# Retention and a PReLU network on one core: attention re-tiled into units of 256 tokens by four heads

## The chip, the cores and the metric

The kernel runs on one NeuronCore of a Trainium2 chip. The metric is the device time of one execution in microseconds (us), the median of several runs. Profiled executions are one run each, and all readings of a trace are from such a run. PE is TensorE (the matrix engine), PEld its weight loads, DVE VectorE, ACT ScalarE, POOL GpSimd and SP SyncE, which here only issues DMAs.

## The reference

Inputs q, k, v are [4 batches, 8 heads, 768 tokens, 64]; w_in is [512, 2048], w_out [2048, 512], alpha [2048]; all float32. For each batch and head a recurrent retention is computed, and its output, heads side by side, goes through a two-layer network:

```python
gamma = 1.0 - 2.0 ** (-5.0 - np.arange(H))
scale = 1.0 / np.sqrt(D)
for t in range(S):
    state = gamma * state + k[t] (outer) v[t]      # per batch and head, 64 x 64
    y[t] = scale * q[t] @ state
x = y laid out as [3072 tokens, 512]
h = x @ w_in
out = (max(h, 0) + alpha * min(h, 0)) @ w_out      # [3072, 512]
```

(The loop is written in short; the index of batch and head is left out.)

## The kernel before, in words

The recurrence is cut into chunks of 128 tokens. Within a chunk the product is a masked attention (scores k.q, mask, times v); from chunk to chunk a 64x64 state per head is carried. A **unit** is one chunk with all eight heads, 24 units in all; four units make a **block** of 512 tokens, six blocks. The network runs block by block.

- `load` (L99, DMA at L104) brings k, q and v of a unit, 256 KB each, 128 tokens on 128 partitions, in pieces of 64 floats (256 bytes), all issued on SP's queue.
- `prep` (L119) scales k (L122) and q (L130) by powers of gamma into float16, and copies v (L142). From unit 10 on, the transposed k and q (tile kq) come from a DMA transpose (L138) on SP's queue; earlier units are transposed on PE (L159) and copied by ACT (L166).
- `stage_a` forms the state sums (L172, tile stp), adds them to the decayed state (L184, or L188 for a batch's first chunk, on DVE) and decays it for the next chunk (L190, POOL, tile tg).
- `stage_b` forms the scores (L205): a head has 64 rows, so two heads' matmuls run on the two row halves of the array, each with 128 columns of weights. DVE masks them (L215, tile m).
- `stage_c` forms the output (L230, L237, and L245 for the carried state, all 128-row products in which half of each weight tile is zero), and ACT copies it into xT (L255).
- `ffn1` (L266) is the first product (L273, 16 tiles of four matmuls with 512 columns), with relu(-h) on ACT (L283, tile hm) and the combination on DVE (L284, tile gt). `ffn2` (L303) is the second (L312, four groups of 16 matmuls), evicted by ACT (L321) and written to the output by a DMA that ACT issues (L325), 128 rows of 2 KB.

The order of the work is written out by hand. Each engine runs its own instructions in program order, and a scheduler doesn't move them. `ffn1` and `ffn2` are generators; `tick(gen, m)` issues the next m of their matmuls, and between ticks the stages of the next block's units are issued. In the steady part (n from 1), the next block's preps and later loads are issued during `ffn1(n)`, its attention during `ffn2(n)`. In the opening, block 0's attention stands alone; `ffn1(0)` starts on three of four units; the weights come through POOL's queue (L384, L388), and the loads of blocks 1 and 2 are held until the second piece of w_out has landed (`held`, L109). `keep_busy` (L328, L332) is 64 small matmuls without use for the result, put before block 1's attention. PSUM has eight banks: four under tag pa, four under tag pb.

Of the kernel before, what the change touches and what calls it, by code (L numbers as in the profile page):

```python
# [9 lines left out]
FP = mybir.dt.float32  # L10
# [8 lines left out]
def kernel(  # L19
# [9 lines left out]
):  # L29
    nc = tc.nc  # L30
# [4 lines left out]
    C = 128  # L35
    NCH = S // C
    NU = B * NCH
    UB = 4
    NBLK = NU // UB
    TB = UB * C  # L40
    scale = 1.0 / np.sqrt(D)
    g64 = 1.0 - 2.0 ** (-5.0 - np.arange(H, dtype=np.float64))
    p_ar = np.arange(128, dtype=np.float64)


# [3 lines left out]
    for h in range(H):  # L49
        tab_np[:, h] = g64[h] ** (127.0 - p_ar)  # L50
        tab_np[:, H + h] = scale * g64[h] ** (p_ar + 1.0 - 128.0)
    for p in range(NP):
        tab_np[0:64, 2 * H + p] = g64[2 * p] ** 128
        tab_np[64:128, 2 * H + p] = g64[2 * p + 1] ** 128
    tab_np[0:NFT, NTAB - 16 : NTAB] = np.eye(NFT)
    tab_np = tab_np.astype(np.float32)
    mi_np = np.zeros((128, 256), dtype=np.float16)
    mi_np[:, 0:128] = p_ar[:, None] <= p_ar[None, :]
    mi_np[:, 128:256] = np.eye(128)
# [9 lines left out]
    mi = sbp.tile([128, 256], F16, tag="mi", name="mi")  # L69
    mask = mi[:, 0:128]  # L70
    ident = mi[:, 128:256]
# [3 lines left out]
    w_in_all = sbp.tile([128, 4, d_ff], F16, tag="win", name="win")  # L75
    w_out_all = sbp.tile([128, NFT, d_model], F16, tag="wout", name="wout")


    NV = 8
    NPE = 10  # L80
    vext = [
        sbp.tile([128, NP, 4, 64], F16, tag=f"vx{i}", name=f"vx{i}")[:, :, 0:3, :]
        for i in range(NV)
    ]

    NT = 2
    sst = [sbp.tile([128, NP, 128], FP, tag=f"ss{i}", name=f"ss{i}") for i in range(NT)]
    tgs = {}

    def ps(name, dt=FP, n=512, tag="pa"):  # L90
        return psp.tile([128, n], dt, tag=tag, bufs=4, name=name)


    staged = {}
    prepped = {}

    held = []

    def load(u):  # L99
        b, c = divmod(u, NCH)  # L100
        t = {}
        for nm, src in (("k", k), ("q", q), ("v", v)):
            t[nm] = sbp.tile([128, H, D], FP, tag=f"{nm}s", bufs=8, name=f"{nm}s{u}")
            ins = nc.sync.dma_start(  # L104
                out=t[nm],
                in_=src[b, :, C * c : C * c + C, :].rearrange("h p d -> p h d"),
            )
            if held:
                tc.add_manual_dep(  # L109
                    ins.ins,  # L110
                    held.pop().ins.name,
                    mybir.DependencyInfo(
                        mybir.DependencyClass.Sync, mybir.DependencyReason.DATA
                    ),
                    reason="loads of the second block after the weights",
                )
        staged[u] = t

    def prep(u, between=None):  # L119
        t = staged.pop(u)  # L120
        kdq = sbp.tile([128, 2, H, D], F16, tag="kdq", bufs=8, name=f"kdq{u}")
        (nc.vector if u < 2 * UB else nc.gpsimd).tensor_tensor(  # L122
            out=kdq[:, 0],
            in0=t["k"],
            in1=tab[:, 0:H].unsqueeze(2).to_broadcast([128, H, D]),
            op=MULT,
        )
        if between:
            between()
        nc.gpsimd.tensor_tensor(  # L130
            out=kdq[:, 1],
            in0=t["q"],
            in1=tab[:, H : 2 * H].unsqueeze(2).to_broadcast([128, H, D]),
            op=MULT,
        )
        kq = sbp.tile([128, 2 * NP, 128], F16, tag="kq", bufs=8, name=f"kq{u}")
        if u >= NPE:
            nc.sync.dma_start_transpose(  # L138
                out=kq, in_=kdq.rearrange("p a h d -> p (a h d)")
            )  # L140
        vx = vext[u % NV]
        nc.gpsimd.tensor_copy(  # L142
            out=vx[:, :, 0::2, :],
            in_=t["v"].rearrange("p (a b) d -> p a b d", b=2),
        )
        prepped[u] = (kdq, kq, vx)


    live = {}
    xT = {}  # L150

    def stage_a(u):
        b, c = divmod(u, NCH)
        kdq, kq, vx = prepped.pop(u)
        kd = kdq[:, 0]
        if u < NPE:
            trb = ps("trb", F16, 1024)
            for p in range(2 * NP):
                nc.tensor.transpose(  # L159
                    out=trb[:, 128 * p : 128 * p + 128],  # L160
                    in_=kdq[:, p // NP, 2 * (p % NP) : 2 * (p % NP) + 2, :].rearrange(
                        "p a d -> p (a d)"
                    ),
                    identity=ident,
                )
            nc.scalar.activation(  # L166
                out=kq.rearrange("p a i -> p (a i)"), in_=trb, func=COPY, bias=0.0, scale=1.0
            )
        if c < NCH - 1:
            stp = ps("stp")  # L170
            for p in range(NP):
                nc.tensor.matmul(  # L172
                    out=stp[:, 128 * p : 128 * p + 128],
                    lhsT=kd[:, 2 * p : 2 * p + 2, :].rearrange("p a d -> p (a d)"),
                    rhs=vx[:, p, 0::2, :],
                    start=True,
                    stop=True,
                )
            new = sst[u % NT]
            stv = stp.rearrange("p (a e) -> p a e", e=128)  # L180
            for lh in range(2):
                s = slice(64 * lh, 64 * lh + 64)
                if c > 0:
                    nc.vector.tensor_tensor(  # L184
                        out=new[s, :, s], in0=tgs[u][s, :, s], in1=stv[s, :, s], op=ADD
                    )
                else:
                    nc.vector.tensor_copy(out=new[s, :, s], in_=stv[s, :, s])  # L188
            tg = sbp.tile([128, NP, 128], F16, tag="tg", bufs=3, name=f"tg{u}")
            nc.gpsimd.tensor_tensor(  # L190
                out=tg,
                in0=new,
                in1=tab[:, 2 * H : 2 * H + NP].unsqueeze(2).to_broadcast([128, NP, 128]),
                op=MULT,
            )
            tgs[u + 1] = tg
        live[u] = (kq.rearrange("p a i -> p (a i)"), vx)

    def stage_b(u):
        kq, vx = live[u]  # L200
        scs = [ps("sca"), ps("scb")]
        for p in range(NP):
            for lh in range(2):
                s = slice(64 * lh, 64 * lh + 64)
                nc.tensor.matmul(  # L205
                    out=scs[lh][:, 128 * p : 128 * p + 128],
                    lhsT=kq[s, 128 * p : 128 * p + 128],
                    rhs=kq[s, 512 + 128 * p : 512 + 128 * p + 128],
                    start=True,
                    stop=True,  # L210
                )
        m2s = []
        for lh in range(2):
            m2 = sbp.tile([128, NP, 128], F16, tag=f"m2{lh}", bufs=2, name=f"m2{lh}")
            nc.vector.tensor_tensor(  # L215
# [282 lines left out]
```

## Time and profile before

| what | value |
|---|---|
| median of 3 runs | 227.44 us (226.75 to 227.81) |
| profiled execution: device time | 227.2 us |
| profiled execution: span, first to last instruction | 225.3 us |
| granted TensorE clock, mean | 1.00 |
| busy, share of span | PE 92%, PEld 48%, DVE 56%, ACT 43%, POOL 37% |
| HBM read / written | 27.39 MB / 6.29 MB |
| first products of blocks 0 and 1 start at | 20.1 us, 62.0 us |

The profile is one execution. Its page gives busy time per engine, the span in 40 slices, the DMA queues (q1 is SP's, q10 is ACT's, q0 is POOL's), the chain of work that ended last (followed back from the last instruction to what released each step), the costliest groups of instructions, and the DMA issues with their time to landing. Further views list one line's instructions, the chain in order of time, and instructions in a window. A group's line reads: source line, engine, operation, output tile <- input tiles, shapes, count | busy us, mean ns of one | idle us before it and what ended it. Matmuls are pipelined: one of 512 columns is shown with some 380 ns, while the next starts 216 ns after it.

### The profile page before, as it was taken

The numbers are of one execution on the slowest core, as the hardware profiler recorded it, in microseconds if no ns is written. First come the engines' busy times: TensorE is split into PE (matmuls) and PEld (weight loads), VectorE is DVE, ScalarE is ACT, GpSimd is POOL, SyncE is SP. The second block draws the span as 40 slices with busy tenths as digits, with TensorE's granted clock in tenths as the row PEclk, the third lists the DMA queues.
The fourth block names the chain that finished last, engine by engine and source line by source line (L and its number), as shares of the span: only waits on it lengthen the run. The fifth ranks groups of instructions, "written<-read, shape, count | busy, mean of one in ns | idle before, by whom it ended". The sixth has DMA issues, their size and how long they took to land.

```text
span 225.3 us, 3831 instructions
## 1 busy us (share of the span) xinstructions
PE 207.7 (92%) x1473; PEld 107.7 (48%) x1473; DVE 125.6 (56%) x202; ACT 96.6 (43%) x156; POOL 83.2 (37%) x98
## 2 busy tenths in 40 slices
PE   1686999589899999999999999999999999999992
PEld 0465544345444555544455544454544555444440
DVE  3594693257368853268954278835288744288000
ACT  2333772123666532276422376232467231576121
POOL 3699300285784026930123980114960220000000
PEclk9999999999999999999999999999999999999999
DMA  7989999999999993999711399941760021100111
GB/s 172 232 182 174 205 202 208 228 242 212 260 291 214 226 236 109 227 255 195 163 47 49 108 245 230 181 126 47 127 155 0 3 79 57 50 3 0 47 68 72
DMA packets 97681, 33.39 MB, mean 148 GB/s; under 512 B 90352, under 2 KB 94592, under 8 KB 97664
## 3 DMA queue, kind: packets, MB, share of 16 engines
q1 hardware_dynamic: 89664, 22.55, 47.4%
q0 software_dynamic: 4224, 4.19, 11.6%
q10 hardware_dynamic: 3776, 6.42, 7.6%
q8 instruction: 11, 0.18, 0.3%
q14 instruction: 6, 0.05, 0.1%
HBM read 27.39 MB, written 6.29 MB: 149 GB/s over the span
## 4 chain that ended last, share of the span: by engine, by line
PE 74%; DMA 11%; POOL 7%; SPq 3%; DVE 1%; issue 1%; ACT 1%; POOLq 0%; DVEq 0%
PE ops L312 33%; PE hps L273 31%; DMA qs<-in_q_dram 5%; DMA wout<-in_moe_w_out_dram 5%; SPq L104 3%; POOL tg L190 3%; PE sca L205 3%; POOL kdq L130 2%; PE yps L237 2%; PE yps L230 2%; PE stp L172 2%; PE yps L245 2%; POOL win L384 1%; POOL vx L142 1%; PE trb L159 1%
## 5 line engine op out<-in xcount | busy, mean ns | idle before, releaser
L312 PE MATMUL ops<-wout,gt 128*128 128x512 f16 x384 | 92.7, 380 | 0.0
L284 DVE SCALAR_TENSOR_TENSOR gt<-hm,oma,hps 128x512 f16<-128x512 f32 x96 | 70.6, 747 | 34.0 <-ACT hm L283 25.1
L273 PE MATMUL hps<-xT,win 128*128 128x512 f16 (+2 forms) x400 | 84.2, 370 | 2.1 <-DMA win<-in_moe_w_in_dram 1.6
L283 ACT ACTIVATE hm<-hps 128x512 f32<-128x512 f32 x96 | 57.0, 597 | 25.1 <-PE hps L273 24.6
L273 PEld LDWEIGHTS <-win 128*128 128x128 f16 x400 | 38.3, 98 | 46.5 <-DMA win<-in_moe_w_in_dram 1.8
L312 PEld LDWEIGHTS <-gt 128*128 128x128 f16 x384 | 34.4, 98 | 34.1
L190 POOL TENSOR_TENSOR tg<-ss,tab 128x512 f16<-128x512 f32 x20 | 21.7, 1084 | 76.6 <-DVE ss L184 53.3
L130 POOL TENSOR_TENSOR kdq<-qs,tab 128x512 f16<-128x512 f32 x24 | 25.2, 1052 | 23.7 <-DMA qs<-in_q_dram 23.7
L215 DVE TENSOR_TENSOR m<-sca,mi 128x512 f16<-128x512 f32 x24 | 16.6, 692 | 27.5 <-PE scb L205 27.3
L321 ACT ACTIVATE os<-ops 128x512 f32<-128x512 f32 x24 | 14.3, 596 | 39.7 <-PE ops L312 39.5
L255 ACT ACTIVATE xT<-yps 128x512 f16<-128x512 f32 x24 | 14.3, 597 | 33.9 <-PE yps L245 28.7
L166 ACT ACTIVATE kq<-trb 128x1024 f16<-128x1024 f16 x10 | 10.2, 1023 | 24.5 <-PE trb L159 24.1
L184 DVE TENSOR_TENSOR ss<-tg,stp 64x256 f32<-64x256 f16 x32 | 13.4, 418 | 9.6 <-PE stp L172 8.3
L237 PE MATMUL yps<-m,vx 128*128 128x128 f16 x96 | 17.0, 223 | 0.4 <-DVE m L215 0.4
L159 PE MATMUL trb<-mi,kdq 128*128 128x128 f16 x80 | 8.3, 246 | 9.8 <-DVE kdq L122 6.1
L230 PE MATMUL yps<-m,vx 128*128 128x128 f16 x96 | 17.1, 223 | 0.0
L122 POOL TENSOR_TENSOR kdq<-ks,tab 128x512 f16<-128x512 f32 x16 | 16.7, 1044 | 0.6 <-DMA ks<-in_k_dram 0.6
L215 DVE TENSOR_TENSOR m<-scb,mi 128x512 f16<-128x512 f32 x24 | 16.3, 681 | 0.0
L142 POOL CAST vx<-vs 128x512 f16<-128x512 f32 x24 | 15.1, 630 | 0.5 <-DMA vs<-in_v_dram 0.5
L245 PE MATMUL yps<-kq,tg 128*128 128x128 f16 x80 | 14.4, 219 | 0.0
L122 DVE TENSOR_TENSOR kdq<-ks,tab 128x512 f16<-128x512 f32 x8 | 6.7, 837 | 10.2 <-DMA ks<-in_k_dram 10.1
L159 PEld LDWEIGHTS <-kdq 128*128 128x128 f16 x80 | 5.9, 108 | 12.7 <-DVE kdq L122 6.2
(25 smaller groups left out, 84.4 us busy)
## 6 DMA issues: line engine op xcount, KB each, us to landing
ks<-in_k_dram SPq DMA_DIRECT2D x24, 256.0 KB, 4.2
qs<-in_q_dram SPq DMA_DIRECT2D x24, 256.0 KB, 4.3
vs<-in_v_dram SPq DMA_DIRECT2D x24, 256.0 KB, 4.7
out_dram<-os ACTq DMA_DIRECT2D x24, 256.0 KB, 2.1
win<-in_moe_w_in_dram POOLq DMA_DIRECT2D x4, 512.0 KB, 6.4
wout<-in_moe_w_out_dram POOLq DMA_DIRECT2D x4, 512.0 KB, 12.6
kq<-kdq SPq DMA_TRANSPOSE x14, 3.8
mi<-mi_const ACTq DMA_DIRECT2D x1, 64.0 KB, 2.8
```

Source lines behind the costliest of these rows:

```text
L122: (nc.vector if u < 2 * UB else nc.gpsimd).tensor_tensor(out=kdq[:, 0], in0=t["k"], in1=tab[:, 0:H].unsqueeze(2).to_broadcast([128, H, D]) ...
L130: nc.gpsimd.tensor_tensor(out=kdq[:, 1], in0=t["q"], in1=tab[:, H : 2 * H].unsqueeze(2).to_broadcast([128, H, D]), op=MULT,)
L142: nc.gpsimd.tensor_copy(out=vx[:, :, 0::2, :], in_=t["v"].rearrange("p (a b) d -> p a b d", b=2),)
L190: nc.gpsimd.tensor_tensor(out=tg, in0=new, in1=tab[:, 2 * H : 2 * H + NP].unsqueeze(2).to_broadcast([128, NP, 128]), op=MULT,)
L215: nc.vector.tensor_tensor(out=m2, in0=scs[lh].rearrange("p (a i) -> p a i", i=128), in1=mask.unsqueeze(1).to_broadcast([128, NP, 128]), op ...
L230: nc.tensor.matmul(out=o, lhsT=vx[:, p, 0:2, :].rearrange("p a d -> p (a d)"), rhs=m2s[0][:, p, :], start=True, stop=False,)
L237: nc.tensor.matmul(out=o, lhsT=vx[:, p, 1:3, :].rearrange("p a d -> p (a d)"), rhs=m2s[1][:, p, :], start=False, stop=(c == 0),)
L245: nc.tensor.matmul(out=o, lhsT=tgs[u][:, p, :], rhs=kq[:, 512 + 128 * p : 512 + 128 * p + 128], start=False, stop=True,)
L273: nc.tensor.matmul(out=hpss[ft][:, lo:hi], lhsT=w_in_all[:, hp, 128 * ft : 128 * ft + 128], rhs=xT[n][:, hp, lo:hi], start=(hp == 0), stop ...
L283: nc.scalar.activation(out=hm, in_=hps, func=RELU, bias=0.0, scale=-1.0)
L284: nc.vector.scalar_tensor_tensor(out=gt[:, ft, :], in0=hm, scalar=oma_sb[:, ft : ft + 1], in1=hps, op0=MULT, op1=ADD,)
L312: nc.tensor.matmul(out=opss[tq], lhsT=gt[:, ft, 128 * tq : 128 * tq + 128], rhs=w_out_all[:, ft, :], start=(ft == 0), stop=(ft == NFT - 1),)
```

## The change

A unit w is now 256 tokens x 4 heads (u, g = divmod(w, 2); g picks the heads), again 24 units and four to a block. Partition p holds tokens 2p and 2p+1, so that a load's pieces are 512 bytes; a unit has two chunks c of 128 tokens (partitions 0 to 63 and 64 to 127) and token parity a. All attention products become 64x64 tiles, four quadrants of the array side by side: row half by column half. Columns of xT come out with the parity ahead of the pair, so that the output rows are written with a stride of two. The zero-padded copy of v and the persistent state tiles go; the decay (was L190, POOL) moves to DVE; in the opening v is copied by ACT. PSUM is split into tags f and p (two banks each) and s and y (one pair of banks each, used whole by transposes, scores and outputs, and as single banks by the first product). Two chunks' carried products into one bank pair are ordered by a wait through a small memset on DVE. Units 8 and 9 are now transposed by DMA. keep_busy and the early part of `ffn1(0)` go. Block 1's first product runs in two halves of 256 tokens.

The diff, cut to its core (line numbers of the kernel after, where they are used, are L140 load, L157 scaling, L187 PE transposes, L213 scores, L231 state sums, L244 mask, L255 and L258 state, L270 carried products, L292 products within, L301 memset, L313 xT, L360 and L381 first product, L405 second, L414 its eviction, L418 output write):

```diff
-    C = 128
-    NCH = S // C
-    NU = B * NCH
-    UB = 4
+    TU = 256
+    NUS = S // TU
+    NW = 2 * B * NUS
+    WB = 4
...
+    NPE = 8
+    def ps_s(name, dt=FP):
+        return ps(name, "s", 1024 if dt == FP else 2048, dt, 1)
...
-                in_=src[b, :, C * c : C * c + C, :].rearrange("h p d -> p h d"),
+                in_=src[b, 4 * g : 4 * g + 4, TU * c3 : TU * c3 + TU, :].rearrange(
+                    "h (p a) d -> p h (a d)", a=2
+                ),
...
+        scaled(nc.vector if opening else nc.gpsimd, 0, t["k"])
+        scaled(nc.gpsimd, 1, t["q"])
...
+        if opening:
+            nc.scalar.activation(out=vx, in_=v_in, func=COPY, bias=0.0, scale=1.0)
+        else:
+            nc.gpsimd.tensor_copy(out=vx, in_=v_in)
...
+    def turn(w):
+        kdq, kq, vx = prepped[w]
+        flat = kdq.rearrange("p k z r d -> p (k z r d)")
+        trb = ps_s("trb", F16)
+        for i in range(8):
+            nc.tensor.transpose(
...
+    DIAG = [(0, 0), (1, 1), (0, 1), (1, 0)]
...
+    def scores(w):
...
+        sc = ps_s("sc")
+        for x in range(2):
+            for a in range(2):
+                for r, c in DIAG:
+                    at = 512 * r + 256 * x + 128 * a
+                    nc.tensor.matmul(
+                        out=sc[half(c), at : at + 128],
+                        lhsT=kq[half(r), 2 * x + a, half(c)],
+                        rhs=kq[half(r), 4 + 2 * x : 6 + 2 * x, half(c)],
...
+    def state_sums(w):
...
+        sums = [ps(f"st{c}", "p") for c in range(1 if last else 2)]
...
+    def after_scores(w):
...
+        for c, stp in enumerate(sums):
+            stv = stp[:, 0:128].rearrange("p (x e) -> p x e", e=D)
+            if c3 + c > 0:
+                new = sbp.tile([128, 2, D], FP, tag="ss", bufs=4, name="ss")
+                nc.vector.tensor_tensor(out=new, in0=tgs[2 * u + c, g], in1=stv, op=ADD)
+                stv = new
+            tg = sbp.tile([128, 4, D], F16, tag="tg", bufs=8, name="tg")[:, 0:2, :]
+            nc.vector.tensor_tensor(out=tg, in0=stv, in1=decay, op=MULT)
...
+    def within(w):
...
+        y = ps("y", "y", 1024, FP, 1)
+        started = set()
+        carried(w, y, started, True)
...
+        done = nc.vector.memset(warm[0:1], 0.0)
+        behind(done, last, "tells that the products within the chunks are through")
+        live[w].append((y, started, done))
+
+    def finish(w):
+        u, g, b, c3 = place(w)
+        y, started, done = live[w].pop()
+        carried(w, y, started, False, done)
...
+    def visit(w_old, w_new):
+        if w_old is not None:
+            within(w_old)
+        if w_new is not None:
+            scores(w_new)
+            state_sums(w_new)
+        if w_old is not None:
+            finish(w_old)
+        if w_new is not None:
+            after_scores(w_new)
...
+    def ffn1(n, order="ffppsSyY"):
...
+    def ffn1_half(n, i, order):
...
-                        nc.scalar.dma_start(out=out[row : row + 128, :], in_=os_sb)
+                        nc.scalar.dma_start(
+                            out=out[row : row + 128, :].rearrange("(p a) m -> a p m", a=2),
+                            in_=os_sb,
+                        )
...
-    def keep_busy():
...
+    prep(0, opening=True)
+    turn(0)
+    prep(1, opening=True)
+    visit(None, 0)
...
+    turn(1)
+    prep(2, opening=True, between=lambda: get_wi(0))
+    visit(0, 1)
+    turn(2)
+    prep(3, opening=True, between=lambda: get_wi(1))
+    visit(1, 2)
+    turn(3)
+    visit(2, 3)
+    get_wi(2)
+    get_wi(3)
     get_wo(0)
...
+    get_wo(1)
+    held.append(get_wo(2))
     get_wo(3)
...
+    visit(3, None)
+    for w in range(WB, 3 * WB):
+        load(w)
+
+    for _ in ffn1(0):
+        pass
+    gen = ffn2(0, parts=4, order="ffyY")
+    tick(gen, 44)
+    prep(4, opening=True)
+    turn(4)
+    tick(gen, 6)
+    prep(5, opening=True)
+    visit(None, 4)
+    tick(gen, 6)
+    turn(5)
     for _ in gen:
         pass
...
+    prep(6, opening=True)
+    visit(4, 5)
+    turn(6)
+    prep(7, opening=True)
+    visit(5, 6)
+    gen = ffn1_half(1, 0, "ffpp")
+    tick(gen, 8)
+    turn(7)
+    tick(gen, 8)
+    visit(6, 7)
+    tick(gen, 16)
+    visit(7, None)
...
+    gen = ffn1_half(1, 1, "ffppsSyY")
+    for i in range(WB):
+        tick(gen, 14)
+        ahead()
...
         gen = ffn2(n)
...
+            tick(gen, 2)
+            visit(None, w0)
+            for i in range(1, WB):
+                tick(gen, 14)
+                visit(w0 + i - 1, w0 + i)
+            tick(gen, 12)
+            within(w0 + WB - 1)
+            tick(gen, 2)
+            finish(w0 + WB - 1)
```

## The prediction, as it went on record

> **What bounds the kernel now.** I read the page's chain of work that ended last first, then that chain in order of time, then the DMA queues and the page's slices.
>
> ```profile
> PE 74%; DMA 11%; POOL 7%; SPq 3%; DVE 1%; issue 1%; ACT 1%; POOLq 0%; DVEq 0%
> ```
> ```profile
> 22.05 11.65 DMA wout<-in_moe_w_out_dram
> ...
> 34.13 7.82 DMA qs<-in_q_dram
> ...
> 61.97 13.97 PE hps L273 x64
> ...
> 95.74 13.81 PE hps L273 x64
> ...
> 128.46 13.81 PE hps L273 x64
> ...
> 160.95 13.81 PE hps L273 x64
> ...
> 193.67 13.81 PE hps L273 x64
> 207.48 13.83 PE ops L312 x64
> 221.33 0.60 ACT os L321
> ```
> The columns are start, length, what. Up to 62 us the chain passes through DMAs, POOL and SP; from there it is TensorE alone, with a tail of 225.3 - 221.3 = 4.0 us. A block's first product takes 13.8 us (64 matmuls of 216 ns), its second as much. What lies between the end of one first product and the start of the next, less 13.83, is attention on TensorE: 5.97, 5.08, 4.85, 5.08, together 20.98 us for blocks 2 to 5 (0.9 of the first is the PE transposes of two units).
>
> **Attention on TensorE.** The nearest row is keep_busy, which has the tiles that the change uses:
>
> ```profile
> L332 PE MATMUL idle<-mi x64: 189/216/243, 38.9 to 40.3; 64*64 64x128 f16 x24, 128*64 128x128 f16 x16, 64*64 64x64 f16 x16, 128*64 128x64 f16 x8
> ```
> Read one by one in the trace, four 64x64 matmuls start within 10 ns, and the next four come 56 ns later at 128 columns, 32 ns at 64. Going from 128-row products into such tiles and back costs about 0.12 + 0.09 = 0.21 us over the plain spacing. A visit then costs: carried rows of the same half 1 group, within 4, scores 4, finish 1, ten groups of 56 ns; state sums 4 of 32 ns: 0.69 us. Before, a unit took 4 stp and up to 12 yps of 55 ns, and 4 pairs of scores of 56 ns: 1.1 us, and one excursion of 0.21. The change makes six excursions a block where there were four (the last unit's within and finish stand apart). Sum per block: 4 x 0.69 + 6 x 0.21 = 4.0 us. To it comes an added wait: finish waits for a memset on DVE that waits for the last product of within. That is 0.22 (matmul's end) + 0.06 + twice some 0.04 = 0.36 us after that product's start; scores and sums, 0.35 us, lie between. Its cost is 0 to 0.36; I take 0.1 (nearer to the covered end). On DVE the memset stands behind m2 and four state products, 2.4 us by the widths of L215 and L184, inside the 14 matmuls (3.0 us) between visits. So 4.3 us a block, **3.8 us saved** over four blocks. The products on 256 tokens of block 1 keep the same columns.
>
> **The opening.** Loads halve their pieces. The page's queues give 47.4% x 225.3 x 16 / 89664 = 19 ns for 256 bytes and about 85 ns for 2048 (writes); a line between gives 28 ns for 512. Twelve loads shrink from 13.1 to some 10 us. But a new chain stands behind them: transposes and scores share one PSUM tile (tag s), so unit after unit runs turn (0.5), ACT copy (1.02, L166), scores (0.5 with latency), m2 (1.25, from 0.69 at half the width), with semaphores 3.3 to 4.0 us. From q scaled at 5.5 us, four units end at 20; with state products, memset, finish and xT (0.6) the first product starts at 22.1 and ends at 36.0, against 34.7 before. Weights are issued earlier (POOL's recurrence products, L190, are gone from its queue) and hide. Then: 13.8 for ffn2(0); 6.5 for four turns, four visits and nine excursions; six waits on kq, m2 or xT with nothing left to fill them, 0.5 to 1.3 us each, 5.5; first product of block 1 in halves, 13.9, with DVE's 32 half products (about 0.45 each by L184's width) pushing 0.8. It ends at 76.5, against 75.94: **0.6 lost**, by -3 to +4. The cold clock at the start (107 ns between 128-column matmuls until 13.8 us) is inside that.
>
> **The output writes.** One line of ffn2 is more than a rename: the write was 128 x 512 on both sides, and is now 2 x 64 x 512 in DRAM (token parity first) against 128 partitions.
>
> ```profile
> q10 hardware_dynamic: 3776, 6.42, 7.6%
> ```
> ```profile
> L325 ACTq DMA_DIRECT2D out_dram<-os x24: 338/338/363, 56.4 to 222.0; - x24
> ...
> DMA to landing us min/median/max: 2.0/2.1/4.8
> ```
> The first line is ACT's DMA queue: packets, MB, share of 16 engines' span. The packets of the last write, one by one: 128 of 2 KB within 0.71 us, eight on each of 16 engines, 80 to 84 ns apart. In the whole trace each DMA's leading counts divide by 16 on both sides (128 rows; 16 for alpha, whose 16 rows are 16 packets), and each closes with 16 completion packets. How a leading count of 2 is shared out no row shows. Bounds: 16 engines, no cost; 2 engines, 64 packets each, 64 x 82 ns = 5.2 us a write. I take 2, since all that the rows show is a split along the leading count, and a split inside it is never seen.
>
> The Trainium skill (DMA: Bandwidth & Descriptors, section "Why a DMA increments its semaphore by 16 and not by 1") says that the descriptor generator takes the slowest dimension that isn't 1 on each side and uses the largest number of engines, up to 16, that divides both. By it the write goes over two engines; no run here shows it yet.
>
> What two engines cost: in the last ffn2 a write comes every 3.46 us and takes 5.2, so they queue. Before, the first one's packets start 4.97 us after that ffn2 starts, and the program ends 1.76 us after the last packet. Now 4.97 + 256 x 0.082 + 1.76 = 27.7 us against 17.8: **9.9 lost**. In the middle blocks both engines have 4 x 5.2 + loads 384 x 28 ns + transposes 256 x 19 ns = 36.5 us of work in a block of 32 us; that lag is carried by six output buffers and a block of lookahead.
>
> **The queue held.** ACT issues these writes itself, in order with its evictions. SP shows what happens to an issue whose engines are behind:
>
> ```profile
> L104 SPq DMA_DIRECT2D vs<-in_v_dram x24: 729/1244/3773, 1.9 to 143.6; - x24
> ```
> Counted in the trace, a load starts free with up to 128 pieces per engine outstanding and is held above that; at the end of a held one 130 to 182 are outstanding. On two engines a write is 64 pieces per engine: the third of a burst reaches the bound, the fourth is held. Block 0's four writes come as a burst (ffn2 in four parts: matmuls 52, 56, 60, 64), from about 49.5 to 53 us, just when transposes and loads of the blocks ahead (15.6 us per engine) are on the same engines; POOL runs ahead of TensorE now. Beside loads a write's packets were 205 ns apart (1.63 us for eight), not 82. With 182 the fourth is released after 256 - 182 = 74 packets: 50.4 + 74 x 0.205 = 65.6 us. Behind it on ACT stand a v copy and xT of unit 4 (0.6 each): 66.8 us in place of 54.6, and within of unit 5 waits for that PSUM tile, TensorE behind it. **12.2 lost**; with 128 it is 23, and nothing if the bound is one for all engines together. I take 182, the row with the mildest bound.
>
> **Sum** against the profiled execution's 227.2 us (span 225.3): 227.2 + 0.6 - 3.8 + 9.9 + 12.2 = **246.1 us**. The median of the runs is 0.24 higher; I leave that.
>
> **Rivals.**
> 1. Two engines, ACT never held: 246.1 - 12.2 = 233.9 us. For it: writes on ACT were never held (338 to 363 ns), and the bound may be on all pieces together, which 128 per write never reaches. Against it: SP's loads were held at a near constant count. 0.27, from 229 to 240.
> 2. Faster: the writes keep 16 engines. 227.2 + 0.6 - 3.8 = 224.0 us, 219 to 229. For it: every write so far used 16; against it: none had so short a leading count. It decides from four engines on: 32 x 82 ns = 2.6 us is under the 3.46 us between writes, the tail then grows by 2 us only and no burst holds ACT. 0.15.
> 3. The tiles don't run four at a time: 0.69 us more a visit, some 14 us over all on top of either case. keep_busy's rows speak against it. 0.06, with all else.
>
> The forecast itself has 0.52, from 238 (a bound reached late, little beside the burst) to 257 (bound 128). The range 229 to 257 leaves out rival 2 and parts of the rest, some 0.19. Of this kernel a measurement tells about 0.5% from no change (226.3 to 228.6). Faster: 0.11, nearly all rival 2. Within: 0.06. Slower: 0.83.
>
> **What will show it.** Time to landing of the output write: some 7 us or more against 2.1 on two engines, else 2.1. ACT's issue of L418 held for many us near 55 to 65, and TensorE idle there, behind xT. The last ffn2's start near 216 with the hold, 204 without, and 24 us more instead of 13.8 + 4.0. Blocks 2 to 5 at 4.3 us of attention; over 5.1 refutes the saving. First product from 22 us. I'm wrong most if the write is split otherwise than by its leading count, or if the opening's single PSUM tile costs far more than its six waits.

## The result, and the profile after

The changed kernel takes **305.96 us** (median of 4 runs, 305.05 to 306.18), against 227.62 us (226.75 to 227.96) for the kernel before on the same chip: ratio 1.344, 95% interval 1.339 to 1.349. The forecast was slower, 246.1 us, within 229 to 257: the sign is right, and 59.9 us are missing. All readings below are from the profiled execution of the kernel named. Three of e3's six executions and two of e9's four took over 1.5% longer than the fastest of the same kernel; the medians below leave them out (238.4 us for e3, where the expectations have the 240.7 of all six), but e3's profiled execution, 244.4 us, is one of them.

The page of the kernel after (span 303.3 us): the chain's shares by engine, and the group of the first product (busy us, mean ns, idle us before it and what ended it).

```profile
PE 57%; DVE 12%; ACT 9%; DMA 8%; SPq 4%; ACTq 2%; issue 2%; POOL 2%; POOLq 0%
...
L360 PE MATMUL hps<-xT,win 128*128 128x512 f16 x320 | 79.8, 403 | 42.1 <-DVE gt L339 39.1
```
Before, the chain was 74% TensorE with 1% of VectorE. Now VectorE has 12% of it, and the first product's matmuls stand idle for 42.1 us (2.1 before), 39.1 of them for VectorE's gt, in twenty waits:

```profile
PE hps L360 <- DVE gt L339: 39.1, 20, 10.6
```
(The columns are us in total, times, longest.) The chain in order of time shows where, here in block 4's first product:

```profile
215.64 4.33 PE hps L360 x20
219.99 0.61 ACT hm L350
220.62 0.76 DVE gt L339
221.42 1.90 PE hps L360 x8
...
224.83 5.35 PE hps L360 x24
...
231.64 1.90 PE hps L360 x8
```
After 20 matmuls (five tiles) TensorE stops until ACT and VectorE have both read the fifth, then 8 matmuls, stop again, 24, stop, 8, stop: four waits of 1.5 us. In the order `ffppsSyY` the sixth tile, S, is the second bank of the pair whose first bank, s, is the fifth tile; the same for Y. The pair is one tile to the program, so a matmul into S waits for the reads of s (e11 puts this to the test). So it goes in the first products of blocks 0 and 2 to 5; block 4's takes 20.4 us where the kernel before has 13.81.

What became of the output writes, from the listing of line 418 (column: duration in ns, min/median/max; then first and last start) and the chain at the end:

```profile
L418 ACTq DMA_DIRECT2D out_dram<-os x24: 522/522/4652, 58.8 to 289.0; - x24
```
```profile
274.55 13.83 PE ops L405 x64
...
288.40 0.60 ACT os L414
```
One issue is held for 4.65 us, that of block 0's last write at 64.43 us. The last second product starts at 274.55 and the span ends at 303.3, 28.8 us later, where it was 17.8. Counted in the trace, a write closes with 2 completion packets of 4 bytes in place of 16 (queue q10 has 96 of them where it had 432), and where no other write is ahead of it, its 128 packets of 2 KB take 6.4 to 6.8 us and the last one ends 7.6 to 8.0 us after the issue, against 1.6 before. And in block 2's first product the chain passes through a DMA of SP's queue (a transpose) into ACT:

```profile
125.20 11.27 DMA kq<-kdq
136.55 0.52 ACTq L418
137.12 0.61 ACT hm L350
```
ACT's write at 136.55 waited for that DMA to land, though its data had been copied by 125.2 us. In the program a write waits for the counter that an earlier DMA used; SP's loads and transposes and ACT's writes share eight counters. All four writes of block 1 stand so: 5.3, 7.0, 4.3 and 11.4 us pass between the end of the copy and the issue, and each issue comes 0.07 to 0.08 us after the last count of the counter's earlier DMA. No later write waits like this. ACT works in order, so the copies hm of the first product stand behind that write, VectorE behind them and TensorE behind VectorE: it is idle for 10.6 us at a stretch here.

The page's row of the granted TensorE clock, in tenths by slice, has dips that the kernel before has nowhere:

```profile
PEclk9999999975999979775699999999999999999985
```
Up to the last second product the clock is half in four stretches, together 34 us, around such idle time (the longest from 132.6 to 149.7 us). There, and at the start of block 0's first product, 32 of the matmuls with 512 columns start 427 ns after the one before in place of 216. That is 6.8 us, so the clock explains little of the loss; before there are none, and in e15, below, nine.

### The profile page after: what moved, and what is told of

Read it like the earlier page. It is cut to its first block, busy times and chain, and to the rows that moved or that the text cites. A ratio compares the mean times of both kernels' runs of the same rounds, so it can differ in the third digit from the quotient of the medians.

```text
span 303.3 us, 5146 instructions
## 1 busy us (share of the span) xinstructions
PE 215.9 (71%) x2145; PEld 109.4 (36%) x2145; DVE 134.1 (44%) x242; ACT 98.6 (33%) x162; POOL 57.9 (19%) x68
## 4 chain that ended last, share of the span: by engine, by line
PE 57%; DVE 12%; ACT 9%; DMA 8%; SPq 4%; ACTq 2%; issue 2%; POOL 2%; POOLq 0%
PE hps L360 24%; PE ops L405 24%; DVE gt L339 10%; ACT hm L350 5%; DMA kq<-kdq 4%; DMA ks<-in_k_dram 3%; PE sc L213 2%; ACTq L418 2%; PE hps L381 2%; SPq L140 2%; ACT kq L192 2%; DVE m L244 2%; PE y L270 2%; SPq L172 2%; DMA vs<-in_v_dram 1%
## 5 line engine op out<-in xcount | busy, mean ns | idle before, releaser
L339 DVE SCALAR_TENSOR_TENSOR gt<-hm,oma,hps 128x512 f16<-128x512 f32 (+1 forms) x112 | 73.1, 670 | 85.8 <-ACT hm L350 82.7
L360 PE MATMUL hps<-xT,win 128*128 128x512 f16 x320 | 79.8, 403 | 42.1 <-DVE gt L339 39.1
L405 PE MATMUL ops<-wout,gt 128*128 128x512 f16 x384 | 90.3, 385 | 2.4 <-ACT os L414 2.4
L360 PEld LDWEIGHTS <-win 128*128 128x128 f16 x320 | 32.6, 102 | 88.2 <-issue 56.8
L405 PEld LDWEIGHTS <-gt 128*128 128x128 f16 x384 | 35.8, 99 | 44.3 <-issue 4.9
L244 DVE TENSOR_TENSOR m<-sc,mi 128x1024 f16<-128x1024 f32 x24 | 29.4, 1223 | 14.4 <-PE sc L213 12.7
L157 POOL TENSOR_TENSOR kdq<-qs,tab 128x512 f16<-128x512 f32 x24 | 25.7, 1071 | 33.9 <-DMA qs<-in_q_dram 33.8
L313 ACT ACTIVATE xT<-y 128x512 f16<-128x512 f32 x24 | 14.3, 596 | 53.0 <-PE y L270 34.7
L157 POOL TENSOR_TENSOR kdq<-ks,tab 128x512 f16<-128x512 f32 x16 | 16.7, 1042 | 61.4 <-PE st L231 40.3
L414 ACT ACTIVATE os<-ops 128x512 f32<-128x512 f32 x24 | 14.3, 596 | 31.9 <-PE ops L405 30.7
L270 PE MATMUL y<-kq,tg 64*64 64x128 f16 x160 | 13.2, 256 | 11.3 <-ACT xT L313 7.7
L381 PE MATMUL hps<-xT,win 128*128 128x256 f16 x128 | 16.0, 281 | 4.5 <-DVE gt L339 3.3
L301 DVE MEMSET warm<- 1x1 f32 x24 | 1.4, 59 | 32.5 <-PE y L292 32.4
L258 DVE TENSOR_TENSOR tg<-ss,tab 128x128 f16<-128x128 f32 x32 | 14.8, 461 | 1.1
L381 PEld LDWEIGHTS <-win 128*128 128x128 f16 x128 | 12.4, 100 | 7.1 <-DVE gt L339 3.9
L270 PEld LDWEIGHTS <-tg 64*64 64x64 f16 x160 | 6.3, 111 | 22.2 <-issue 15.4
L187 PE MATMUL trb<-mi,kdq 128*128 128x128 f16 x64 | 7.3, 279 | 9.5 <-DVE kdq L157 4.5
L213 PE MATMUL sc<-kq 64*64 64x128 f16 x384 | 11.3, 241 | 2.6 <-ACT kq L192 2.6
L192 ACT ACTIVATE kq<-trb 128x1024 f16<-128x1024 f16 x8 | 8.2, 1023 | 14.0 <-PE trb L187 13.4
L292 PE MATMUL y<-m,vx 64*64 64x128 f16 x384 | 11.8, 240 | 0.0
```

What stands on the lines that cost most here:

```text
L157: eng.tensor_tensor(out=kdq[:, kind].rearrange("p z r d -> p r z d"), in0=src.rearrange("p (r x) (a d) -> p r (x a) d", a=2, x=2), in1=tab ...
L213: nc.tensor.matmul(out=sc[half(c), at : at + 128], lhsT=kq[half(r), 2 * x + a, half(c)], rhs=kq[half(r), 4 + 2 * x : 6 + 2 * x, half(c)], ...
L244: nc.vector.tensor_tensor(out=m2.rearrange("p s a i -> p s (a i)"), in0=sc.rearrange("p (s n) -> p s n", n=256), in1=mask.unsqueeze(1).to_ ...
L258: nc.vector.tensor_tensor(out=tg, in0=stv, in1=decay, op=MULT)
L270: ins = nc.tensor.matmul(out=y[half(x), 512 * c + 128 * r : 512 * c + 128 * r + 128], lhsT=tgs[2 * u + c, g][half(r), x, :], rhs=kq[half(r ...
L313: nc.scalar.activation(out=xT[n][:, 2 * g : 2 * g + 2, TU * i : TU * i + TU].rearrange("p r (c i) -> p c r i", c=2), in_=y.rearrange("p (c ...
```

## The experiments

Theory at the outset: the miss is (a) the bank pairs in the first product and (b) the slow write, which costs more than its tail. Rivals: the waits at the pairs are a symptom of late ACT and VectorE, not of the pairs; the write costs only its tail; or a third cause is the larger. All times are medians, as said above; "before" is run beside each.

| run | us | ratio to before, 95% |
|---|---|---|
| after | 305.96 | 1.339 to 1.349 |
| e1 single banks | 276.62 | 1.205 to 1.225 |
| e2 write cut in two | 277.86 | 1.210 to 1.231 |
| e3 both | 238.42 (six runs, 237.96 to 244.43) | 1.041 to 1.056 |
| e4 before, with the new write (rows in another order) | 268.80 | 1.170 to 1.191 |
| e5 single banks, natural order | 234.39 | 1.024 to 1.036 |
| e6 e3, block 1 whole | 239.50 | 1.048 to 1.057 |
| e7 e3, transposes apart | 240.08 | 1.049 to 1.060 |
| e8 e5, with the edits of e6 and e7 | 232.89 | 1.019 to 1.031 |
| e9 e8, block 1 woven | 236.93 (four runs, 235.56 to 241.34) | none given |
| e10 e9, later sums | 235.66 | 1.034 to 1.044 |
| e11 after, first banks of the pairs only | 279.96 (one run) | - |
| e12 e1, writes from POOL | 251.31 (one run) | - |
| e13 e10, 8 writes from POOL | 232.31 | 1.017 to 1.025 |
| e14 e8, 8 writes from POOL | 249.68 | 1.092 to 1.100 |
| e15 e13, units ahead | 225.46 | 0.987 to 0.993 |
| e16 e15, 4 writes from POOL | 238.81 | 1.045 to 1.053 |

### The bank pairs: e1 and e11

```diff
-    def ffn1(n, order="ffppsSyY"):
+    def ffn1(n, order="ffpp"):
...
-    gen = ffn1_half(1, 1, "ffppsSyY")
+    gen = ffn1_half(1, 1, "ffpp")
```


> The first product takes its PSUM banks from tags f and p alone (four single banks), not also from the pairs s and y; all else as in the kernel after. Theory A (bank pairs): in the trace of after, TensorE stops four times in each first product of blocks 0 and 2 to 5, 1.5 to 1.7 us each, at the second bank of a pair until DVE has read the first; the first product takes 20.4 to 21.9 us there. Without pairs it takes 13.8 to 14.2, five times 7 us and some 3 in block 1 go: 306 becomes 262 to 275. Rival B (slower clock or slower matmuls, granted clock 0.93): the stops only mirror an engine that is slow anyway, and the time stays above 295.

e1 takes 276.62 us, 29.3 less, just above the range of theory A, with half as many PSUM banks for the first product. Its granted clock is no higher, 0.91 in the mean for 0.93, so rival B, with its time above 295, falls. In its chain the products of blocks 3 to 5 run without a gap:

```profile
168.09 13.81 PE hps L360 x64
...
200.02 13.83 PE hps L360 x64
...
232.74 13.81 PE hps L360 x64
```
e11 keeps both pairs in use, but only their first banks (`"ffppsy"`):

> The changed kernel, its write on two engines left as it is, with six PSUM tiles in the first product instead of eight: the four single banks and the first bank of each pair, the second banks left unused. Theory (a matmul into the second bank of a pair waits because the pair is one tile, whose first bank VectorE is still reading): with no second bank nothing waits, the first product takes 13.8 us in blocks 2 to 5, and the time is that of four single banks, 272 to 281 us. Rival (any use of the two pairs in the first product is late, since scores and outputs of the attention hold them): a wait stays at the first use of each pair, the product takes 15 us or more and the time is 284 to 300.

```profile
L360 PE MATMUL hps<-xT,win 128*128 128x512 f16 x320 | 75.7, 399 | 11.5 <-DVE gt L339 8.8
```
It takes 279.96 us. Of the twenty waits of L360 for gt one is left, of 8.8 us, in block 2's product, behind ACT's held write. So it is neither the number of banks nor the use of the attention's banks, but the second bank of a pair that is one tile.

### The write: e2, e3, e4 and e12

```diff
-                        nc.scalar.dma_start(
-                            out=out[row : row + 128, :].rearrange("(p a) m -> a p m", a=2),
-                            in_=os_sb,
-                        )
+                        rows = out[row : row + 128, :].rearrange("(p a) m -> a p m", a=2)
+                        for a in range(2):
+                            nc.scalar.dma_start(out=rows[a], in_=os_sb[64 * a : 64 * a + 64])
```


> Each output write is issued as two DMAs of 64 rows from 64 partitions, so that the leading count is 64 on both sides; all else as in the kernel after. Theory C (two engines): the write then lands in some 2 to 3 us instead of 6.5, the stretch from the last second product's start to the end falls from 28.8 to 18 us, and the waits of ACT's writes in blocks 0 to 2 go (4.7 us in block 0's burst, some 18 to 22 in block 2, where first product and writes of block 1 stand behind DMAs on the same engines): 306 becomes 268 to 278. Rival D (the loads of 512-byte pieces and the transposes are late by themselves): only the tail goes, 293 to 297.

e2 takes 277.86 us: 28.1 less, for the same rows to the same places, only with a leading count of 64 in each write. From the start of the last second product to the end it is 18.6 us again, and each half of a write lands in 2.2 to 2.4 us where nothing is ahead of it. The tail's 10 us are so less than half of what the slow write costs. With both edits:

> Both edits of the two other kernels. Theories A and C: what the prediction's rival 2 described is left, with the opening as measured (first product from 23.8 us): 221 to 228. If there is a third cause in blocks 0 to 2, 232 or more.

238.4 us. The two edits add more than singly (the write's alone is worth 28.1 us beside the pairs and 38.2 without them), but 11 us to the kernel before stay: a third cause. e4 puts the new write into the kernel before, without the new order of xT's columns, so that its output rows land in another order than the reference's:

```diff
-                        nc.scalar.dma_start(out=out[row : row + 128, :], in_=os_sb)
+                        nc.scalar.dma_start(
+                            out=out[row : row + 128, :].rearrange("(p a) m -> a p m", a=2),
+                            in_=os_sb,
+                        )
```


> The kernel before, with the output write alone in the new form (2 x 64 x 512 in DRAM); its rows are thereby written in another order. Theory C: landing of 5.5 us or more, a tail longer by 10 us, and waits of ACT or SP behind slow writes in the blocks with loads: 238 to 258. If the write's form costs nothing by itself: 227 to 229. If it costs the tail alone, 236 to 239.

268.8 us, 41 more than before and more than any theory gave. Its tail is 28.8 us too; the rest goes with the hold of ACT, in the chain twice, as in the kernel after:

```profile
95.82 12.08 DMA ks<-in_k_dram
...
110.94 5.18 DMA ks<-in_k_dram
116.19 0.52 ACTq L325
116.81 0.61 ACT hm L283
```
Here a load takes 12 us to land (4.2 to 4.7 in the median of the kernel before). ACT's writes at 94.48, 111.03 and 116.19 us are each issued 0.08 us after the landing of the DMA that used their counter, with the first product's copies behind them. e12 takes the slow writes out of ACT's queue (e1 with one word changed: `nc.gpsimd.dma_start`):

> The changed kernel with four single banks (276.6 us) and its output writes, in the same form, issued by GpSimd instead of ScalarE. Theory (in blocks 1 to 3 the slow write costs by holding ScalarE, in whose queue the copies of the first product wait behind the write's issue): ScalarE has no hold left, the first product of block 2 is no longer interrupted, and the time falls by 12 to 25 us, to 252 to 265, while the end stays about 28 us behind the start of the last second product. Rival (the slow writes hold up the loads themselves, on the two engines that carry both, whoever issues them): the second product of block 2 still starts after 140 us (149 with ScalarE) and the time is 270 to 280. GpSimd's own scaling work can be held by the issues in its turn, which would show as waits of its own.

251.31 us, 25.3 less than e1, a little more than expected. The second product of block 2 starts at 126 us in place of 149. Its writes still land in 9.4 us, and from the start of the last second product to the end it is 26 us. Loads and transposes land hardly sooner for it: they take up to 8.4 and 9.8 us, and in e1's chain, where ACT stands behind them, 8.2 and 9.9. So most of what the slow write costs beyond its tail goes with ACT held in its own queue, not with the loads being late for the attention. One thing besides the queue differs, and its share is not separated: GpSimd's writes go as 64 packets of 4 KB, with 448 of 8 bytes, in place of 128 of 2 KB.

### What is left: e5, e6, e7 and e8

e5 has single banks, and the copy out of PSUM puts the tokens in natural order, so that the write is the old one:

```diff
+        for c in range(2):
+            lo = TU * i + 128 * c
             nc.scalar.activation(
-                out=xT[n][:, 2 * g : 2 * g + 2, TU * i : TU * i + TU]...
+                out=xT[n][:, 2 * g : 2 * g + 2, lo : lo + 128].rearrange(
+                    "p r (i a) -> p r a i", a=2
+                ),
...
+                        nc.scalar.dma_start(out=out[row : row + 128, :], in_=os_sb)
```


> The changed kernel with the first product on four single PSUM banks, and with the tokens put back into natural order by the copy out of PSUM (two copies of 128x256 in place of one of 128x512), so that an output write is again one write of 128 rows in their order. Theory (what the slow write cost was the two engines, whoever cures it): the 128-row write lands in about 2.5 us, last second product to the end 18 to 19 us, and with half as many write issues in ACT's queue as in the kernel with the write cut in two (240.7 us), 233 to 241 us. Rival (cutting the write only hid part of it, the longer ACT work of the two copies, 24 of about 0.35 us more, or the order of rows itself costs): over 244 us.

234.39 us, and 17.7 us for the tail. It is 4.0 us under e3 with half as many writes in ACT's queue: block 2's first product, 18.7 us in e3's trace, is no longer interrupted (14.0). What remains is 10 us over the forecast's sum without the write (224.0). Most of it is lost before block 1's second product, whose first matmul starts at 83.3 us here, against 76.5 before (the starts below are counted so; the 90.9 that the expectations give for e3 is where its unbroken part begins). So two edits on the front part, e6 and e7, each on e3, and both on e5, e8:

> The kernel with both cures (single banks, write cut in two; 240.7 us) and block 1's first product made whole, after all four of its attention units, as blocks 2 to 5 have it, in place of two halves of 256 tokens. Theory (block 1 is late by 9 us because its 64 pieces of gt of 256 elements keep VectorE busy 0.44 us each, 28 us, where 16 pieces of 512 take 12): block 1's second product starts near 84 to 87 us in place of 90.9 and the time falls to 234 to 237. Rival (block 1 is late because its attention runs one unit after the other behind block 0's four output copies and their write issues on ACT, and no first product beside it covers that): the second product starts at 90 to 94 and the time is 240 to 244.

> The kernel with both cures (240.7 us) and the opening's four transposes in the PSUM banks of the feed-forward (free then) in place of the one pair that holds the scores too. Theory (the opening is late because a unit's transposes wait until VectorE has read the scores of the unit before): the four units go at about 2.9 us or less in place of 4.1, the first product starts at 20 to 22 us in place of 24.1, and the time falls by 2 to 3 us. Rival (what starts block 1 is the arrival of its inputs behind the weights, so that an earlier first product is only idle later): first product earlier, time within 1 us of 240.7.

> Single banks, natural order with one plain write, block 1's first product whole, opening transposes apart: all of the cures so far. If they add, 226 to 233 us, at or above the kernel before (227.6); if the order of the work in block 1 (its attention behind the end of block 0's second product) is the largest thing left, 234 to 240, with block 1's second product at 86 us or later (75.9 before).

e6 (block 1's first product after all its units, `ffn1(1)` in place of the halves) starts block 1's second product at 87.3 us, and its time, 239.5, lies between what the two theories gave and is not below e3's 238.4. The theory's count was off besides: the trace has 32 pieces of gt of 256 elements, 14.0 us in all, not 64 and 28. e7 (`trb` in tag f for units 0 to 3) starts the first product at 21.7 us in place of 24.0 as expected, but its time, 240.08, isn't below e3's either; with e3's scatter that settles little. The cleaner pair is e8 against e5: first product 2.2 us earlier, block 1's second product only 0.8 earlier (82.5), the time 1.5 lower with overlapping intervals, just inside the 226 to 233 expected of cures that add. The opening's single tile and the halves are not where the 10 us go. What block 1 waits for shows in e3's chain there:

```profile
58.75 0.49 ACTq L420
59.23 0.05 issue
59.28 0.60 ACT os L414
59.89 0.04 issue
59.93 0.32 PE y L270 x4
```
The attention's first output of block 1 (y) starts when ACT has copied the last of block 0's second product out of the pair of y: with order `ffyY` that product holds the pair to its end, and unit after unit then runs alone. How much of block 1's lateness this order makes is not isolated: e9 and e14, below, met other waits.

### The order of block 1, and ACT's hold: e9, e10, e13 and e14

e9 makes block 0's second product bank by bank and weaves block 1's units into it:

```diff
-    gen = ffn2(0, parts=4, order="ffyY")
-    tick(gen, 44)
+    gen = ffn2(0)
+    tick(gen, 18)
     prep(4, opening=True)
     turn(4)
...
+    tick(gen, 12)
     visit(4, 5)
     turn(6)
...
+    tick(gen, 10)
     visit(6, 7)
```


> The kernel with all cures so far (232.9 us; its second product of block 1 starts at 82.5 to 84.4 us, 75.9 to 76.5 in the kernel before), with block 0's second product made bank by bank, on the two feed-forward banks, and block 1's attention woven into it, unit by unit, as the later blocks do it. Theory (what is left of the loss is the order of block 1's work, where the attention stands behind the second product since that holds the bank pair of y): block 1's second product starts at 72 to 77 us and the time falls to 220 to 226, at or below the kernel before. Rival (block 1 waits for its inputs behind the weights, or for the second weight's last quarter, whatever the order): second product of block 1 at 80 us or later and 229 to 234.

It is slower than e8, 236.9 us, with block 1's second product at 87.7. That theory, as it stood, fell, and so did its rival, since the inputs were there (unit 5's had landed by 41.6 us):

```profile
46.25 4.56 DMA ks<-in_k_dram
50.89 0.36 ACTq L418
51.30 0.63 ACT vx L177
```
Bank by bank, block 0's first write comes early, in the middle of SP's twelve loads, and waits for a load's counter until 50.89, 9.3 us after its copy; unit 5's copies are behind it. e10 moves the first scores and state sums of blocks 2 to 5 six matmuls later (`tick(gen, 8)` before the first visit, 8 instead of 14 after it):

> The kernel with block 1 woven, and in blocks 2 to 4 the first scores and state sums placed six matmuls later in the second product, so that the state sums no longer wait for the bank that VectorE reads last of the first product (1.4 to 1.6 us of idle TensorE at the border of two products in three of the blocks). If that wait is on the path: 2.5 to 4.5 us below the kernel with block 1 woven. If the wait only moves on to the next product: within 1 us of it.

1.3 us less than e9, inside e9's scatter. From the start of block 1's second product to the end, where the edit acts, e10's trace is 1.7 us shorter than e9's (147.1 for 148.8): less than the 2.5 to 4.5 expected of the waits at the border of two products, more than the rival's 1. e13 and e14 have the writes of blocks 0 and 1 on POOL's queue, woven and unwoven:

```diff
-                        nc.scalar.dma_start(out=out[row : row + 128, :], in_=os_sb)
+                        (nc.gpsimd if n < 2 else nc.scalar).dma_start(out=out[row : row + 128, :], in_=os_sb)
```


> The woven kernel with later sums (235.7 us), with the eight output writes of blocks 0 and 1 issued by GpSimd instead of ScalarE, blocks 2 to 5 as before. Theory (weaving lost because the first write of block 0 stands in ScalarE's queue until 50.9 us, for the semaphore of a load that SyncE issued behind it, with the copies of block 1's second unit behind the write; the same hold, 6 us, interrupts block 2's first product at 102 to 109): both holds go, block 1's second product starts at 74 to 79 us in place of 86.2, and the time is 219 to 226. Rival (block 1's inputs land too late for any order): the second product of block 1 at 83 us or later, 230 to 236.

> The kernel with the three cures together (232.9 us; block 1's attention behind block 0's second product), with the writes of blocks 0 and 1 issued by GpSimd. If the place of block 1's attention is what costs once no write holds ScalarE, this stays well behind the woven kernel with the same writes: block 1's second product at 80 to 83 us, 226 to 231 us in all. If the hold was the whole loss, both start it within 1.5 us of one another and are equally fast.

In e13 block 1's second product starts at 78.1 us, inside the theory's 74 to 79; the time is 232.31, outside its 219 to 226, since 6 us are lost again later: block 3's units stand in POOL's queue behind block 1's writes until 97.8 us. e14 is at 91 us there, and at 249.68 in all, later than either theory had it, for a reason that neither named:

```profile
L258 DVE TENSOR_TENSOR tg<-ss,tab x32: 291/292/10994, 10.8 to 213.1; 128x128 f16<-128x128 f32 x32
```
One decay of 0.29 us took 10.99, from 56.2 to 67.2 us, while POOL ran nine scalings and four copies one right after the other. So e14 doesn't isolate the order of block 1, as it was meant to.

### The waits taken away: e15 and e16

```diff
+        if n == 1:
+            for i in range(WB):
+                ahead()
         gen = ffn2(n)
```


> The woven kernel with GpSimd's writes for blocks 0 and 1 (232.3 us), with block 3's units scaled one block earlier, ahead of block 1's writes in GpSimd's queue. Theory (with block 1 mended, the only loss left is 6 us in blocks 2 and 3, where the units of block 3 stood in GpSimd's queue behind block 1's writes until 97.8 us although their inputs had landed, and their transposes then held ScalarE's write until 133.9): the second product of block 3 starts at 141 to 143 us in place of 148.5, and the time is 222 to 226.5, at or below the kernel before (227.7). Rival (the units one block ahead fill the eight buffers, and the transposes or the loads wait elsewhere): 228 us or more.

> The same, with block 1's writes back on ScalarE and only block 0's four on GpSimd. If ScalarE's hold at its writes comes from loads that are late because the units' scaling is late, it is gone here too and the time is within 1.5 us of the run with eight writes on GpSimd. If the semaphores shared with the loads hold ScalarE whatever the loads' lead, block 2's first product is interrupted for 4 to 6 us and the time is 3 to 6 us above it.

e15 takes **225.46 us** (224.72 to 226.05, 6 runs), ratio 0.990 to the kernel before (0.987 to 0.993): without the waits, and with block 1 in another order, the kernel with the changed attention is 2.2 us faster than the kernel before, clear of the scatter but only 1%. The kernel before was not run with GpSimd's writes or with its units ahead, so how much of the 2.2 us is the attention's is not separated. From block 1's second product on, its chain is TensorE alone:

```profile
78.74 1.73 PE ops L405 x8
...
97.12 13.81 PE hps L360 x64
110.94 1.73 PE ops L405 x8
...
129.01 13.81 PE hps L360 x64
142.82 1.73 PE ops L405 x8
...
160.82 13.81 PE hps L360 x64
174.63 1.73 PE ops L405 x8
...
192.70 13.81 PE hps L360 x64
206.52 13.83 PE ops L405 x64
```
e16 differs only in the queue of block 1's four writes, ACT's again, and takes 238.81, 13.4 more, where 3 to 6 were expected of the hold. Its chain:

```profile
91.60 4.46 DMA ks<-in_k_dram
96.14 0.35 ACTq L418
```
ACT's write of block 1 waits again for a load, and the first product of block 2 behind it; block 2's second product starts at 123.1 us, against 110.8 in e15. The four writes are issued 4.3, 5.5, 1.5 and 8.2 us after their copies, each 0.07 to 0.08 us after the last count of its counter; the third waits so for ACT's own write that was held before it. This pair is the cleanest evidence for the shared counters: same products, same order, same data.

## Why the prediction was wrong, point by point

Two steps failed: the first product was carried over without a wait at the bank pairs, and the hold of ACT was put down to one burst, where most of it came from counters shared with the loads.

- **The write on two engines** was right: 2 completion packets, the last packet 7.6 us after the issue (some 7 forecast), a tail of 28.8 us for 27.7. The section of the Trainium skill that the prediction cited (DMA: Bandwidth & Descriptors, "Why a DMA increments its semaphore by 16 and not by 1") is borne out by this trace; it also says that a DMA issued by GpSimd has all 16 engines count whatever its shape, and e12's writes of the same shape close with 16 packets each.
- **"The queue held", 12.2 us**, was the wrong mechanism in the main. The fourth issue was held 4.65 us. The larger part came at the four writes of block 1, which the counters shared with SP's loads and transposes held for 27.9 us; the step left these out. e4 (+41 us for the write alone, 11 of it tail) and e12 (-25.3 us) put the cost near 25 to 30 us. The write cost 28.1 us in this kernel, 38.2 once the pairs are cured, for 9.9 + 12.2 = 22.1 forecast.
- **"A block's first product takes 13.8 us"** was carried from the kernel before with no term for the new banks. This step failed worst: 20.4 to 22.0 us in blocks 0 and 3 to 5, 29.3 us in all (e1), 39.4 with the write cured (e2 to e3). The trace of before holds no such wait, but in the changed kernel s and S are halves of one tile, and e11 shows that the wait goes by the tile.
- **The opening, 0.6 us.** The first product starts at 23.8 us for 22.1. "Six waits, 5.5 us" took block 0's second product as filler for block 1's units; that product held the pair of y, and ACT's queue had its copies and writes first. Block 1's second product starts 7 to 11 us late with the write cured (e5, e6), for 0.6 forecast; in e15 it is 2.1 us late. That the opening's single tile would cost far more than its waits, named as a danger, is not borne out: taking the transposes out of it brings the first product 2.3 us forward (e7).
- **Attention, 4.3 us a block, 3.8 saved**, was right. In e15, between the end of a first product and the next one's start, less 13.83: 4.55, 4.24, 4.17, 4.24, together 17.2 us, against 20.98 before. In the kernel after itself blocks 3 to 5 show it too, 4.2 us each; only block 2's stretch is longer, 10.7 us, with ACT's hold in it.
- **The sum without the write**, rival 2's 224.0 us, is near what e15 measures, 225.5, once the new waits are gone. The closeness is in part luck, since e15 has another order of block 1's work and other queues. The attention's and the slow write's own times were right and the waits weren't. The path there in order: 305.96, single banks -29.3, write cut -38.2, natural order instead -4.0, the two small edits -1.5, weaving with POOL's writes and units ahead -7.4. The shares depend on that order, since the waits cover one another.

## What to carry to other kernels

When a diff changes how PSUM is cut into tiles, go through the unchanged loops that use it and ask of each matmul which reads it must now wait for, by whole tiles. A slower DMA is priced at what waits for its counter, in every queue, not only at the end of the kernel. And an engine that issues DMAs between its own steps stands still whenever an issue waits; POOL's queue took that from ACT, as long as POOL's own work was ahead of the writes.

## What the runs showed of the hardware

- Work on GpSimd can hold up VectorE for long. The state's decay, 0.29 us, took 0.92 to 1.18 us in five places of the kernel after, where POOL scaled beside it, and 10.7 us in e12 and 10.99 us in e14, in each while thirteen scalings and copies of POOL followed one another without a pause; no such row is in the kernel before, where POOL made the decay itself. The Trainium skill (Trainium Architecture — The Big Picture, "What this means for kernel authors") says that the two share a port pair under an exclusive lock, which agrees with these rows.
- The clock can come late to the first matmuls. After the opening's small products, the first 7 of block 0's first product in the kernel after and the first 11 in e3 started some 427 ns apart, then 216; the trace grants the full clock there from 26.8 and 29.0 us on. In the kernel before it was full from 14.0 us, ahead of the first product's start at 20.1.
